# A decode-step kernel (cached attention, then a gated MLP): three buffers for K and V in place of two, a new order of the first loads, and the weights loaded at the end into freed K and V buffers

## Chip, cores, metric

One core of one Trainium2 chip. The metric is device time in microseconds (us), the median of repeated executions. The profile's span is 1.7 to 1.9 us shorter than the time of the same execution. Sums below are made on the spans of the profiled executions unless "time" is said; runs of one kernel differ by 0.2 to 2.2 us, so tenths of a span are worth something only beside a wait that shows the same.

## The reference

```python
# x: 2 x 1 x 512; k_cache, v_cache: 2 x 32 heads x 8192 x 128, bf16
q = (layernorm(x) @ wq)                       # 2 x 32 heads x 128
p = softmax(q . k_cache / sqrt(128))          # over 8192 positions
h = x + (p . v_cache) @ wo                    # wo: 4096 x 512
h2 = h + (relu(ln(h) @ W_gate) * (ln(h) @ W_up)) @ W_down   # 512 x 1376, 1376 x 512
```

K and V are 64 (batch, head) pairs of 2.097 MB each: 268 MB of the 281.7 MB that a run moves. Everything else is small, and comes in smaller rows.

## The kernel before

A pair ("head" below) has its scores computed on VectorE: a product of the K tile (128 partitions x 64 positions x 128) with q, then six halving additions and one last one. ScalarE takes the exponential, TensorE the weighted sum with V. SyncE issues K and the weights on one DMA queue, ScalarE issues V on another.

```python
kt = [sbuf(f"kt{i}", [128, J, Dh]) for i in range(2)]      # two buffers of K; vt the same
...
for i in range(2): dma_v(i)                                # ScalarE's queue
for b in range(B): nc.sync.dma_start(xT[:, :, b], ...)     # x: 1024 elements of 2 bytes
dma_wq_chunk(0); dma_k(0); dma_wq_chunk(1); dma_k(1)       # SyncE's queue
for k in range(2, NWQ): dma_wq_chunk(k)                    # 8 chunks of 0.5 MB, 1 KB rows
...                                                        # layer norm, first q
for i in range(NH):                                        # 64 heads
    nc.vector.wait_ge(kdone[par], 16 * (i // 2 + 1))
    ...
    if i % GH == 1 and g + 1 < NG: emit_q_group_dve(g + 1) # q of 4 heads, PSUM -> SBUF, VectorE
    nc.vector.tensor_tensor(out=prod[:], in0=kt[par][:], in1=qb, op=ALU.mult).then_inc(multdone, 1)
    if i + 2 < NH:
        nc.sync.wait_ge(multdone, i + 1)
        dma_k(i + 2)
        if 2 <= i < 2 + NWT:                               # wo, Wg, Wu, Wd0, Wd1 at heads 2 to 6
            weights_list[i - 2][1]().then_inc(sem_wend, 16)
    ...                                                    # halving tree -> scores
    nc.scalar.activation(out=e_t[par][:], in_=scores[par][:], func=ACT.Exp, ...).then_inc(expdone, 1)
    if i + 2 < NH:
        nc.scalar.wait_ge(pvdone, i + 1)
        dma_v(i + 2)
    ...                                                    # 64 matmuls with V
...                                                        # wo, layer norm, MLP, output
```

The softmax here doesn't subtract the row's maximum and nothing guards it: scores larger than these inputs give would overflow.

## Time and profile before

| | before |
|---|---|
| time, median | 727.66 us (727.13 to 728.16, 13 runs) |
| span of the profiled run | 725.6 us |
| first product starts | 22.74 us |
| last score ends | 705.89 us |
| waits of VectorE for K in the loop | 22.3 us |

The lines on which the reading rests are in the prediction. Two more views. The chain that ended last, shares of the span by engine:

```profile
DVE 80%; DMA 12%; SPq 4%; issue 2%; PE 2%; DVEq 0%; ACT 0%
```

### The profile page before, as it was taken

The page shows a single profiled execution, that of the slowest core. Times are in us where ns is not written, and L with a number is a line of the kernel's source. Part 1 is how long each engine was busy: PE and PEld are TensorE (multiplying, and loading weights), DVE is VectorE, ACT ScalarE, POOL GpSimd, SP SyncE. Part 2 cuts the span into 40 slices and gives each one's busy share as a digit, 9 for nine tenths or more (in the row PEclk, how much of TensorE's full clock was granted, in tenths as well). Part 3 has the DMA queues.
Part 4 walks back from the last instruction along what each step waited for, and adds up shares of the span by engine and source line. Part 5 has one row for each costly group of instructions (what it writes and reads, how often), then busy time and mean ns, then how long its engine had stood idle before and what let it go on. Part 6 is the DMA issues. An engine that isn't in the chain of part 4 may idle for free.

```text
span 725.6 us, 9928 instructions
## 1 busy us (share of the span) xinstructions
PE 158.7 (22%) x4433; PEld 130.2 (18%) x4433; DVE 645.6 (89%) x570; ACT 26.6 (4%) x133; POOL 0.7 (0%) x6
## 2 busy tenths in 40 slices
PE   0312111222123212321323132212321232112216
PEld 0101101112112111210212021201211121111115
DVE  0899188999999999999999999999999999999982
ACT  0000000000000000000000000000000000000010
POOL 0000000000000000000000000000000000000000
DMA  8999999999999999999999999999999999999930
GB/s 342 380 429 396 408 411 411 424 407 399 410 394 416 390 425 385 422 416 391 412 405 421 396 402 406 411 402 403 411 399 426 379 424 406 400 409 399 417 144 3
DMA packets 30348, 281.70 MB, mean 388 GB/s; under 512 B 3329, under 2 KB 12897, under 8 KB 13921
## 3 DMA queue, kind: packets, MB, share of 16 engines
q1 hardware_dynamic: 21088, 146.84, 48.7%
q10 hardware_dynamic: 9216, 134.22, 46.3%
q8 instruction: 35, 0.57, 0.3%
q14 instruction: 9, 0.07, 0.0%
HBM read 281.05 MB, written 0.00 MB: 387 GB/s over the span
## 4 chain that ended last, share of the span: by engine, by line
DVE 80%; DMA 12%; SPq 4%; issue 2%; PE 2%; DVEq 0%; ACT 0%
DVE tb L342 40%; DVE prod L323 36%; DMA kt<-in_A_k_cache_dram 12%; SPq L183 2%; DVE scores L351 2%; SPq L190 1%; DVE qgrp L220 1%; PE work L401 0%; PE work L368 0%; PE work L442 0%; DVEq L319 0%; PE work L448 0%; PE work L471 0%; SPq L241 0%; PE work L386 0%
## 5 line engine op out<-in xcount | busy, mean ns | idle before, releaser
L323 DVE TENSOR_TENSOR prod<-kt,qgrp 128x8192 bf16<-128x8192 bf16 x64 | 283.2, 4426 | 10.0 <-DMA kt<-in_A_k_cache_dram 3.5
L368 PE MATMUL work<-e,vt 128*128 128x1 bf16 x4096 | 119.5, 165 | 539.7 <-ACT e L356 539.7
L368 PEld LDWEIGHTS work<-e,vt 128*128 128x128 bf16 x4096 | 114.2, 104 | 557.3 <-ACT e L356 557.3
L342 DVE TENSOR_TENSOR tb<-tb 128x2048 bf16<-128x2048 bf16 (+4 forms) x320 | 183.0, 572 | 10.9
L342 DVE TENSOR_TENSOR tb<-prod 128x4096 bf16<-128x4096 bf16 x64 | 146.7, 2292 | 2.2
L356 ACT ACTIVATE e<-scores 128x64 bf16<-128x64 f32 x64 | 16.4, 256 | 664.7 <-DVE scores L351 664.7
L209 PE MATMUL qps<-wq_sb,xrep 128*128 128x512 bf16 x64 | 29.9, 623 | 4.5 <-DVEq L297 3.4
L220 DVE CAST qgrp<-qps 128x512 bf16<-128x512 f32 x16 | 11.1, 691 | 22.3 <-DMA kt<-in_A_k_cache_dram 18.8
L351 DVE TENSOR_TENSOR scores<-tb 128x64 f32<-128x64 bf16 x64 | 14.4, 225 | 2.2
L256 DVE CAST xT_f<-xT 128x8 f32<-128x8 bf16 x1 | 0.2, 171 | 14.1 <-DMA xT<-in_A_x_dram 14.1
L356 ACT ACTIVATION_READ_ACCUMULATOR e<-scores 128x1 f32 x64 | 11.9, 186 | 0.0
L209 PEld LDWEIGHTS qps<-wq_sb,xrep 128*128 128x128 bf16 x64 | 6.9, 128 | 14.3 <-issue 8.8
L262 PE MATMUL work<-xT_f,ones_f 128*128 128x8 f32 x2 | 0.6, 370 | 15.5 <-DVE xsq L258 15.5
L401 PE MATMUL work<-O_sb,wo_sb 128*128 128x2 bf16 x128 | 3.6, 165 | 0.6 <-DVEq L395 0.6
L401 PEld LDWEIGHTS work<-O_sb,wo_sb 128*128 128x128 bf16 x128 | 3.5, 104 | 0.8 <-DVEq L395 0.8
L406 DVE TENSOR_TENSOR hT_f<-work,xT_f 128x8 f32<-128x8 f32 x1 | 0.2, 166 | 3.7 <-PE work L401 3.7
L262 PEld LDWEIGHTS work<-xT_f,ones_f 128*128 128x128 f32 x2 | 0.5, 313 | 15.5 <-DVE xsq L258 15.5
L453 DVE COPY u_sb<-work 128x20 f32<-128x20 f32 x1 | 0.2, 179 | 3.1 <-PE work L448 3.1
L382 DVE RECIPROCAL zinv<-work 1x64 f32<-1x64 f32 x1 | 0.5, 546 | 2.6 <-PE work L378 2.6
L442 PE MATMUL work<-hnT,Wg_sb 128*128 128x2 bf16 (+1 forms) x44 | 1.5, 170 | 2.2 <-DVEq L436 2.2
L442 PEld LDWEIGHTS work<-hnT,Wg_sb 128*128 128x128 bf16 (+1 forms) x44 | 1.5, 112 | 2.3 <-DVEq L436 2.3
L448 PE MATMUL work<-hnT,Wu_sb 128*128 128x2 bf16 (+1 forms) x44 | 1.5, 170 | 0.0
(55 smaller groups left out, 21.3 us busy)
## 6 DMA issues: line engine op xcount, KB each, us to landing
vt<-in_A_v_cache_dram ACTq DMA_DIRECT2D x64, 2048.0 KB, 12.6
kt<-in_A_k_cache_dram SPq DMA_DIRECT2D x64, 2048.0 KB, 12.9
wq_sb<-in_A_wq_dram SPq DMA_DIRECT2D x8, 512.0 KB, 14.4
wo_sb<-in_A_wo_dram SPq DMA_DIRECT2D x1, 4096.0 KB, 39.0
Wg_sb<-in_B_W_gate_dram SPq DMA_DIRECT2D x1, 1376.0 KB, 19.5
Wu_sb<-in_B_W_up_dram SPq DMA_DIRECT2D x1, 1376.0 KB, 21.0
Wd_sb<-in_B_W_down_dram SPq DMA_DIRECT2D x1, 1280.0 KB, 19.6
Wd_sb<-in_B_W_down_dram SPq DMA_DIRECT2D x1, 96.0 KB, 19.9
```

The lines of the kernel that those rows point to most:

```text
L183: return nc.sync.dma_start(wq_sb[:, :, k * GW:(k + 1) * GW], A_wq[:, k * GW:(k + 1) * GW].rearrange("(c p) n -> p c n", p=128),).then_inc( ...
L190: return nc.sync.dma_start(kt[i % 2][:], A_k_cache[b, h].rearrange("(p j) d -> p j d", p=128)).then_inc(kdone[i % 2], 16)
L209: last = nc.tensor.matmul(qps[:, slot * 512:slot * 512 + GW], lhsT=xrep[:, b_g * DC + c, :], rhs=wq_sb[:, c, col0:col0 + GW], start=(c == ...
L220: dve.run(nc.vector.tensor_copy(out=q_grp[slot][:], in_=qps[:, slot * 512:slot * 512 + GW]))
L323: nc.vector.tensor_tensor(out=prod[:], in0=kt[par][:], in1=qb, op=ALU.mult).then_inc(multdone, 1)
L342: dve.run(nc.vector.tensor_tensor(out=out_ap, in0=cur_in[:, :, 0:half], in1=cur_in[:, :, half:cur_w], op=ALU.add))
L351: nc.vector.tensor_tensor(out=scores[par][:], in0=cur_in[:, :, 0:1].rearrange("p j o -> p (j o)"), in1=cur_in[:, :, 1:2].rearrange("p j o ...
L356: nc.scalar.activation(out=e_t[par][:], in_=scores[par][:], func=ACT.Exp, scale=inv_sqrt_dh, accum_out=ZP[:, col:col + 1]).then_inc(expdon ...
L368: last = nc.tensor.matmul(O_ps[:, col:col + 1], lhsT=vt[par][:, j, :], rhs=e_t[par][:, j:j + 1], start=(j == 0), stop=(j == NJ - 1))
L401: last = nc.tensor.matmul(attnT_ps[:, ncx * B:(ncx + 1) * B], lhsT=wo_sb[:, h, ncx * 128:(ncx + 1) * 128], rhs=O_sb[:, h, :], start=(h == ...
L442: last = nc.tensor.matmul(g_ps[0:fw, fc * B:(fc + 1) * B], lhsT=Wg_sb[:, c, fc * 128:fc * 128 + fw], rhs=hnT[:, c, :], start=(c == 0), sto ...
L448: last = nc.tensor.matmul(u_ps[0:fw, fc * B:(fc + 1) * B], lhsT=Wu_sb[:, c, fc * 128:fc * 128 + fw], rhs=hnT[:, c, :], start=(c == 0), sto ...
```

## The change

Intent: let the DMA engines run further ahead, keep the early part free of weights that are needed only at the end, and let x and K0 come first. V is issued one head ahead up to head 20 and two ahead afterwards. Wg, Wu and Wd have no memory of their own any more: they are loaded into K and V buffers that are free at the end.

```diff
+    NB = 3                                   # kt, vt, kdone, vdone: i % NB in place of i % 2
-                for i in range(min(2, NH)):
-                    dma_v(i)
                 (x)
                 dma_wq_chunk(0)
                 dma_k(0)
-                if NWQ > 1: dma_wq_chunk(1)
-                if NH > 1: dma_k(1)
-                for k in range(2, NWQ): dma_wq_chunk(k)
+                dma_wq_chunk(1)
+                dma_k(1)
+                dma_wq_chunk(2)
+                dma_k(2)
                 (layer norm)
+                nc.scalar.wait_ge(kdone[0], 16)
+                dma_v(0)
 (loop)
-                    if i + 2 < NH:
+                    if i + NB < NH:
                         nc.sync.wait_ge(multdone, i + 1)
-                        dma_k(i + 2)
-                        if 2 <= i < 2 + NWT:
-                            weights_list[i - 2][1]().then_inc(sem_wend, 16)
+                        dma_k(i + NB)
+                        if i % 4 == 1 and 3 + i // 4 < NWQ: dma_wq_chunk(3 + i // 4)
+                        if i == 60: (wo).then_inc(sem_wo, 16)
 (exponential)
+                    if i >= 2: nc.scalar.wait_ge(pvdone, i - 1)      # before the exponential
-                    if i + 2 < NH:
-                        nc.scalar.wait_ge(pvdone, i + 1)
-                        dma_v(i + 2)
+                    if i < 20: dma_v(i + 1)
+                    elif i == 20: dma_v(i + 1); nc.scalar.wait_ge(pvdone, i); dma_v(i + 2)
+                    elif i + 2 < NH: nc.scalar.wait_ge(pvdone, i); dma_v(i + 2)
 (after the loop)
+                nc.sync.wait_ge(multdone, NH - 2); (Wg into kt of head 61)
+                nc.sync.wait_ge(multdone, NH - 1); (Wu into kt of head 62)
+                nc.sync.wait_ge(pvdone, NH - 2);   (Wd into vt of head 61)
```

More of the change, by code (lines that the diff above doesn't have):

```diff
@@ L61, in bass_sequential_preLN__gqa_block_cached__glu_gated_reglu__decode_kernel @@
     qdim = Hq * Dh
-    GH = 4
-    assert Hq % GH == 0
+    GH = 4 if Hq % 4 == 0 else Hq
     NGB = Hq // GH
@@ L73, in bass_sequential_preLN__gqa_block_cached__glu_gated_reglu__decode_kernel @@
         sem_x = S("x")
-        sem_wq2 = None
-        sem_wend = S("wend")
+        sem_wo = S("wo")
+        sem_wgu = S("wgu")
+        sem_wd = S("wd")
         sem_prep = S("prep")
@@ L80, in bass_sequential_preLN__gqa_block_cached__glu_gated_reglu__decode_kernel @@
         sem_qcopied = S("qcopied")
-        kdone = [S("kdone0"), S("kdone1")]
-        vdone = [S("vdone0"), S("vdone1")]
+        kdone = [S(f"kdone{k}") for k in range(NB)]
+        vdone = [S(f"vdone{k}") for k in range(NB)]
         multdone = S("multdone")
@@ L110, in bass_sequential_preLN__gqa_block_cached__glu_gated_reglu__decode_kernel @@
         dve = EngChain(nc.vector, dvesem)
-        kt = [es.enter_context(nc.sbuf_tensor(f"kt{i}", [128, J, Dh], BF16)) for i in range(2)]
-        vt = [es.enter_context(nc.sbuf_tensor(f"vt{i}", [128, J, Dh], BF16)) for i in range(2)]
+        kt = [es.enter_context(nc.sbuf_tensor(f"kt{i}", [128, J, Dh], BF16)) for i in range(NB)]
+        vt = [es.enter_context(nc.sbuf_tensor(f"vt{i}", [128, J, Dh], BF16)) for i in range(NB)]
         wq_sb = es.enter_context(nc.sbuf_tensor("wq_sb", [128, DC, qdim], BF16))
@@ L117, in bass_sequential_preLN__gqa_block_cached__glu_gated_reglu__decode_kernel @@
         wo_sb = es.enter_context(nc.sbuf_tensor("wo_sb", [128, Hq, D], BF16))
-        Wg_sb = es.enter_context(nc.sbuf_tensor("Wg_sb", [128, DC, F], BF16))
-        Wu_sb = es.enter_context(nc.sbuf_tensor("Wu_sb", [128, DC, F], BF16))
-        Wd_sb = es.enter_context(nc.sbuf_tensor("Wd_sb", [128, FC, D], BF16))
         ones_f32 = es.enter_context(nc.sbuf_tensor("ones_f32", [128, 128], F32))
@@ L150, in bass_sequential_preLN__gqa_block_cached__glu_gated_reglu__decode_kernel @@
         e_t = [es.enter_context(nc.sbuf_tensor(f"e{i}", [128, J], BF16)) for i in range(2)]
+        if DC * F <= J * Dh and FC * D <= J * Dh and NH >= 3:
+            alias_w = True
+            pstride = kt[0][:].ap[0]
+            wg_view = bass.AP(kt[(NH - 3) % NB], 0, [[pstride[0], 128], [F, DC], [1, F]])
+            wu_view = bass.AP(kt[(NH - 2) % NB], 0, [[pstride[0], 128], [F, DC], [1, F]])
+            wd_view = bass.AP(vt[(NH - 3) % NB], 0, [[pstride[0], 128], [D, FC], [1, D]])
+        else:
+            alias_w = False
+            wg_t = es.enter_context(nc.sbuf_tensor("wg_sb", [128, DC, F], BF16))
+            wu_t = es.enter_context(nc.sbuf_tensor("wu_sb", [128, DC, F], BF16))
+            wd_t = es.enter_context(nc.sbuf_tensor("wd_sb", [128, FC, D], BF16))
+            wg_view = wg_t[:]
+            wu_view = wu_t[:]
+            wd_view = wd_t[:]
         qps = es.enter_context(nc.psum_tensor("qps", [128, 2 * 512], F32))
@@ L168, in bass_sequential_preLN__gqa_block_cached__glu_gated_reglu__decode_kernel @@
         sem_wq = [S(f"wq{k}") for k in range(NWQ)]
-        weights_list = [
-            ("wo", lambda: nc.sync.dma_start(wo_sb[:], A_wo.rearrange("(h d) n -> d h n", d=128))),
-            ("Wg", lambda: nc.sync.dma_start(Wg_sb[:], B_W_gate.rearrange("(c p) f -> p c f", p=128))),
-            ("Wu", lambda: nc.sync.dma_start(Wu_sb[:], B_W_up.rearrange("(c p) f -> p c f", p=128))),
-        ]
         nfull = F // 128
         frem = F - nfull * 128
-        weights_list.append(("Wd0", lambda: nc.sync.dma_start(
-            Wd_sb[:, 0:nfull, :], B_W_down[0:nfull * 128, :].rearrange("(c p) n -> p c n", p=128))))
-        if frem:
-            weights_list.append(("Wd1", lambda: nc.sync.dma_start(Wd_sb[0:frem, nfull, :], B_W_down[nfull * 128:F, :])))
-        wend_total = 16 * len(weights_list)
         def dma_wq_chunk(k):
@@ L190, in dma_k @@
             return nc.sync.dma_start(
-                kt[i % 2][:], A_k_cache[b, h].rearrange("(p j) d -> p j d", p=128)
-            ).then_inc(kdone[i % 2], 16)
+                kt[i % NB][:], A_k_cache[b, h].rearrange("(p j) d -> p j d", p=128)
+            ).then_inc(kdone[i % NB], 16)
         def dma_v(i):
@@ L196, in dma_v @@
             return nc.scalar.dma_start(
-                vt[i % 2][:], A_v_cache[b, h].rearrange("(p j) d -> p j d", p=128)
-            ).then_inc(vdone[i % 2], 16)
+                vt[i % NB][:], A_v_cache[b, h].rearrange("(p j) d -> p j d", p=128)
+            ).then_inc(vdone[i % NB], 16)
         def emit_q_group_pe(g):
@@ L245, in _ @@
                 dma_k(0)
-                if NWQ > 1:
-                    dma_wq_chunk(1)
-                if NH > 1:
-                    dma_k(1)
-                for k in range(2, NWQ):
-                    dma_wq_chunk(k)
+                dma_wq_chunk(1)
+                dma_k(1)
+                dma_wq_chunk(2)
+                dma_k(2)
                 dve.run(nc.vector.memset(ones_f32[:], 1.0))
@@ L305, in _ @@
                 NJ = J
-                NWT = len(weights_list)
                 for i in range(NH):
                     b, h = divmod(i, Hq)
+                    buf = i % NB
                     par = i % 2
@@ L312, in _ @@
                     gslot = g % 2
-                    if i % GH == 0 and 1 <= g + 1 < NG and i > 0:
-                        pass
-                    nc.vector.wait_ge(kdone[par], 16 * (i // 2 + 1))
+                    nc.vector.wait_ge(kdone[buf], 16 * (i // NB + 1))
                     if i >= 1:
@@ L323, in _ @@
                     nc.vector.tensor_tensor(
-                        out=prod[:], in0=kt[par][:], in1=qb, op=ALU.mult).then_inc(multdone, 1)
-                    if i + 2 < NH:
+                        out=prod[:], in0=kt[buf][:], in1=qb, op=ALU.mult).then_inc(multdone, 1)
+                    if i + NB < NH:
                         nc.sync.wait_ge(multdone, i + 1)
-                        dma_k(i + 2)
-                        if 2 <= i < 2 + NWT:
-                            weights_list[i - 2][1]().then_inc(sem_wend, 16)
+                        dma_k(i + NB)
+                        if i % 4 == 1 and 3 + i // 4 < NWQ:
+                            dma_wq_chunk(3 + i // 4)
+                        if i == 60:
+                            nc.sync.dma_start(wo_sb[:], A_wo.rearrange("(h d) n -> d h n", d=128)).then_inc(sem_wo, 16)
                     nc.vector.wait_ge(multdone, i + 1)
@@ L336, in _ @@
                         half = cur_w // 2
-                        buf = tb1 if toggle == 0 else tb2
-                        out_ap = buf[:, 0:J * half].rearrange("p (j w) -> p j w", w=half)
+                        bt = tb1 if toggle == 0 else tb2
+                        out_ap = bt[:, 0:J * half].rearrange("p (j w) -> p j w", w=half)
                         if not first:
@@ L355, in _ @@
                     nc.scalar.wait_ge(sready, i + 1)
+                    if i >= 2:
+                        nc.scalar.wait_ge(pvdone, i - 1)
                     nc.scalar.activation(
@@ L358, in _ @@
                         accum_out=ZP[:, col:col + 1]).then_inc(expdone, 1)
-                    if i + 2 < NH:
-                        nc.scalar.wait_ge(pvdone, i + 1)
+                    if i < 20:
+                        dma_v(i + 1)
+                    elif i == 20:
+                        dma_v(i + 1)
+                        nc.scalar.wait_ge(pvdone, i)
+                        dma_v(i + 2)
+                    elif i + 2 < NH:
+                        nc.scalar.wait_ge(pvdone, i)
                         dma_v(i + 2)
@@ L364, in _ @@
                     nc.tensor.wait_ge(expdone, i + 1)
-                    nc.tensor.wait_ge(vdone[par], 16 * (i // 2 + 1))
+                    nc.tensor.wait_ge(vdone[buf], 16 * (i // NB + 1))
                     last = None
@@ L368, in _ @@
                         last = nc.tensor.matmul(
-                            O_ps[:, col:col + 1], lhsT=vt[par][:, j, :], rhs=e_t[par][:, j:j + 1],
+                            O_ps[:, col:col + 1], lhsT=vt[buf][:, j, :], rhs=e_t[par][:, j:j + 1],
                             start=(j == 0), stop=(j == NJ - 1))
                     last.then_inc(pvdone, 1)
-                n_emitted = max(0, min(NWT, NH - 4))
-                for w in range(n_emitted, NWT):
-                    weights_list[w][1]().then_inc(sem_wend, 16)
+                if alias_w:
+                    nc.sync.wait_ge(multdone, NH - 2)
+                nc.sync.dma_start(wg_view, B_W_gate.rearrange("(c p) f -> p c f", p=128)).then_inc(sem_wgu, 16)
+                if alias_w:
+                    nc.sync.wait_ge(multdone, NH - 1)
+                nc.sync.dma_start(wu_view, B_W_up.rearrange("(c p) f -> p c f", p=128)).then_inc(sem_wgu, 16)
+                if alias_w:
+                    nc.sync.wait_ge(pvdone, NH - 2)
+                nc.sync.dma_start(
+                    wd_view[:, 0:nfull, :], B_W_down[0:nfull * 128, :].rearrange("(c p) n -> p c n", p=128)
+                ).then_inc(sem_wd, 16)
+                wd_total = 16
+                if frem:
+                    nc.sync.dma_start(wd_view[0:frem, nfull, :], B_W_down[nfull * 128:F, :]).then_inc(sem_wd, 16)
+                    wd_total = 32
                 nc.tensor.wait_ge(expdone, NH)
@@ L396, in _ @@
                 nc.tensor.wait_ge(sem_osb, 1)
-                nc.tensor.wait_ge(sem_wend, wend_total)
+                nc.tensor.wait_ge(sem_wo, 16)
                 last = None
@@ L437, in _ @@
                 nc.tensor.wait_ge(sem_hn, 1)
+                nc.tensor.wait_ge(sem_wgu, 32)
                 last = None
@@ L442, in _ @@
                         last = nc.tensor.matmul(
-                            g_ps[0:fw, fc * B:(fc + 1) * B], lhsT=Wg_sb[:, c, fc * 128:fc * 128 + fw],
+                            g_ps[0:fw, fc * B:(fc + 1) * B], lhsT=wg_view[:, c, fc * 128:fc * 128 + fw],
                             rhs=hnT[:, c, :], start=(c == 0), stop=(c == DC - 1))
@@ L448, in _ @@
                         last = nc.tensor.matmul(
-                            u_ps[0:fw, fc * B:(fc + 1) * B], lhsT=Wu_sb[:, c, fc * 128:fc * 128 + fw],
+                            u_ps[0:fw, fc * B:(fc + 1) * B], lhsT=wu_view[:, c, fc * 128:fc * 128 + fw],
                             rhs=hnT[:, c, :], start=(c == 0), stop=(c == DC - 1))
@@ L466, in _ @@
                 nc.tensor.wait_ge(sem_hd, 1)
+                nc.tensor.wait_ge(sem_wd, wd_total)
                 last = None
@@ L471, in _ @@
                         last = nc.tensor.matmul(
-                            yT_ps[:, ncx * B:(ncx + 1) * B], lhsT=Wd_sb[0:fw, fc, ncx * 128:(ncx + 1) * 128],
+                            yT_ps[:, ncx * B:(ncx + 1) * B], lhsT=wd_view[0:fw, fc, ncx * 128:(ncx + 1) * 128],
                             rhs=hd[0:fw, fc * B:(fc + 1) * B], start=(fc == 0), stop=(fc == FC - 1))
```

## The prediction

> **What bounds the kernel now.** I read the page first: busy shares and slices. Format of the rows: tenths of each slice that an engine was busy, 40 slices of 18.1 us.
>
> ```profile
> PE 158.7 (22%) x4433; PEld 130.2 (18%) x4433; DVE 645.6 (89%) x570; ACT 26.6 (4%) x133; POOL 0.7 (0%) x6
> ...
> DVE  0899188999999999999999999999999999999982
> ...
> DMA  8999999999999999999999999999999999999930
> GB/s 342 380 429 396 408 411 411 424 407 399 410 394 416 390 425 385 422 416 391 412 405 421 396 402 406 411 402 403 411 399 426 379 424 406 400 409 399 417 144 3
> ```
>
> VectorE and the DMA engines are both full nearly everywhere. VectorE has three holes: slice 1, slices 5 to 7, and the end. DMA has none until the last 30 us. Next, the groups by shape, for what one head costs on VectorE:
>
> ```profile
> L323 DVE TENSOR_TENSOR prod<-kt,qgrp 128x8192 bf16<-128x8192 bf16 x64 | 283.2, 4426 | 10.0 <-DMA kt<-in_A_k_cache_dram 3.5
> L342 DVE TENSOR_TENSOR tb<-prod 128x4096 bf16<-128x4096 bf16 x64 | 146.7, 2292 | 2.2
> L342 DVE TENSOR_TENSOR tb<-tb 128x2048 bf16<-128x2048 bf16 x64 | 78.3, 1224 | 2.2
> ```
>
> With the five smaller steps (692, 425, 292, 226, 225 ns) a head is 9.80 us of work; the distance from one product to the next in the timeline is 10.13 us, and 10.97 us when a group of q is copied first (15 times inside the loop). So the loop without waits is 64 x 10.13 + 15 x 0.84 = 660.9 us. The waits of VectorE (us in total, times, longest) say what is added:
>
> ```profile
> DVE qgrp L220 <- DMA kt<-in_A_k_cache_dram: 18.8, 2, 18.5
> DVE xT_f L256 <- DMA xT<-in_A_x_dram: 14.1, 1, 14.1
> ...
> DVE prod L323 <- DMA kt<-in_A_k_cache_dram: 3.5, 2, 2.4
> ```
>
> The first product starts at 22.74 and the last score ends at 705.89: 683.15 us, which is 660.9 plus 22.3 of waits for K. The two holes have their cause in the timeline (start, duration[...]):
>
> ```profile
> 0.74 1.00 SPq L241 DMA_DIRECT2D xT<-in_A_x_dram  x2
> 0.75 1.00 ACTq L196 DMA_DIRECT2D vt<-in_A_v_cache_dram  x2
> ...
> 2.32 9.17 SPq L190 DMA_DIRECT2D kt<-in_A_k_cache_dram  x1
> ...
> 15.12 0.17 DVE L256 CAST xT_f<-xT 128x8 f32<-128x8 bf16 x1 [14.12 <-DMA xT<-in_A_x_dram]
> ...
> 59.48 18.07 SPq L190 DMA_DIRECT2D kt<-in_A_k_cache_dram  x1
> ...
> 93.72 0.69 DVE L220 CAST qgrp<-qps 128x512 bf16<-128x512 f32 x1 [18.52 <-DMA kt<-in_A_k_cache_dram]
> ```
>
> x (1024 packets of 2 bytes) is issued together with two V loads and lands only at 15; K of head 5 stands behind wo (4 MB in 1 KB rows, issued at 49.7) and its issue alone takes 18 us. Last, the same counters over long stretches (last two columns: DMA share, GB/s):
>
> ```profile
> 140.00:570.00 430.00, 95.13 (x2668) 76.89 (x2665) 414.71 (x341) 14.30 (x82) 0.00 (x0) 1.00 0.99 406
> 35.00:60.00 25.00, 5.55 (x136) 3.93 (x132) 23.26 (x18) 0.70 (x4) 0.00 (x0) 1.00 1.01 425
> ```
>
> In the steady part VectorE sets the pace: four heads take 3 x 10.13 + 10.97 = 41.36 us and ask for 8 x 2.097 MB, 406 GB/s, which is what DMA delivers. When both queues have a backlog it delivers 425. So the reserve of the DMA engines is some 4%, no more: that is the number on which this case turns.
>
> **What the Trainium skill says.** "DMA: Bandwidth & Descriptors", section "Queues, rings and completion order": each DMA engine goes round between the queues that have work, a packet at a time. The packet records agree: between 3 and 13 us each half microsecond starts about 12 packets of V (16 KB, 611 ns) and about 12 of x (2 bytes, 9 ns), one for one; in the half microsecond after V ended, 396 packets of x start. So a queue with small packets is slowed to the pace of the big ones beside it. The section "Issuing engines are not separate DMA queues" says that queues of different engines share the same 16 DMA engines; the trace agrees, the sum never goes past some 440 GB/s. "HBM Reference", "Specifications", says that a core streaming alone measures about 425 GB/s, bounded by its DMA engines; the 425 above agrees. "Perfetto Trace Analysis", "Identifying the Most-Contended Engine", calls the occupancy of 16 DMA engines misleading; here too, since 0.99 busy goes with 406 and with 425.
>
> **The change part by part.** No instruction of VectorE, TensorE or ScalarE is added or removed: the order of instructions per engine is the same but for DMA issues. What changes is when 281.7 MB are asked for, and in how many buffers.
>
> *Start.* V0 and V1 no longer go ahead of x; V0 waits for K0. x is then alone: the records show 59 packets in its first quarter microsecond and 88 in the next half, before V came in full; at about 250 per us, 1024 take 4 us from 1.8, so it is through at 6 and lands at 7. From x's landing to the first product the old kernel needs 22.74 - 15.12 = 7.6 us (layer norm, q), so 14.4. K0: wq0 takes 1.6 us (some 170 packets of 1 KB each half us), K0 5.2 us, landing 0.7: 6 + 7.5 = 13.5, in time. First product at about 14.4 in place of 22.7: 8.4 us gained, all on the path.
>
> *The hole at 75 to 94.* wo, Wg, Wu, Wd (8.3 MB) leave the early heads, and five of eight wq chunks are spread over heads 1 to 17. The 22.3 us of K waits go with the queue that made them. But the reserve is thin. Four heads and a wq chunk are 16.8 MB at 420 GB/s, 39.9 us, and 1.5 us for the chunk: 41.4 against VectorE's 41.36. So in the first 17 heads there is no lead to be built, and whatever is short at the start stays: K1 and V0 share the engines, then wq2 stands among V1's packets one for one (up to 5 us during which K does not move), then K2: I follow K1 to land at 24.0 (wanted at 24.5), K2 at 36.4 (35.5), K5, behind wq3, at 69.5 (66.7). Together I set 4 us of new waits. Triple buffers do not add bandwidth; they only let K be asked for 10 us earlier, so they absorb a late one such as the K of 16 us at 577 in the old kernel (0.3 us of wait there).
>
> *Steady part.* VectorE-bound as before, 41.36 us per four heads. The lead grows by about 0.2 to 0.4 us a head, so by head 60 K is its full two to three buffers ahead. Nothing gained, nothing lost. The new wait of the exponential for the weighted sum two heads back is no new wait in time: the sum follows the exponential within 2.5 us.
>
> *Tail.* wo is issued after the product of head 60 (time T), Wg, Wu, Wd after it into freed K and V buffers. Scores of head 63 end at T + 5.7 + 30.4 + 0.8 = T + 36.9. Old tail: from score end 705.9 to wo's first matmul 4.6 us, to Wg's 11.9, to Wd's 15.5, to the end 19.7. So wanted: wo T + 41.5, Wg and Wu T + 48.8, Wd T + 52.4. To be moved from T on, in time of the engines: rest of K62 1 to 5 us, K63 5, rest of V61 3, V62 and V63 5 each, wo 13 (256 rows of 1 KB per engine at 51 ns), Wg and Wu 3.5 each (109 ns a row), Wd 4.4: 43 to 48 us. Add 2 for issue and landing: wo at T + 34 to 40, Wu at T + 41 to 46, Wd at T + 45 to 50. They arrive just in time; I set 1.5 us for lateness.
>
> *Sum.* 727.4 - 8.4 - 22.3 + 4 + 1.5 = 702.2 us.
>
> **The rivals.** *DMA becomes the bound.* Two floors lie close: VectorE's 14.4 + 660.9 + 19.7 = 695.0 us of span, and DMA's: 6 us of start, then 281.7 MB, at 425 GB/s 663 and at 406 694 us, then 5.7 us from Wd's last byte to the end: 675 to 706. If the true rate with both queues always full is nearer 406 (the steady part never showed whether it could go faster), the holes come back as small waits for K all along, and the time is some 708. For it: DMA share 0.99 over 430 us. Against: 425 to 440 in several 5 us windows, and no wait for K over 48 heads with double buffers. *The weights come late at the end*: at 406 GB/s the tail's reserve is gone and TensorE waits 3 to 9 us for Wg or Wd: 705 to 710. *The start does not gain*: if x, 2 bytes a packet, is slow by itself, the first product stays near 20 and the time is 708. *K's queue is starved by its own wq chunks* in heads 2 to 17: 8 us more than I set, 710. Against the last: what V takes early it does not take later, since V is issued one head at a time.
>
> **Range and chances.** All rivals but a combination of two end under 712.9, which is 2% faster. Low end: no new waits at all, 696. High end: one rival in full and half of another, 711. Faster by over 2%: 0.93; within 2%: 0.06; slower: 0.01.
>
> **What would show it.** x landing near 7 and the first product near 14.4 show the start right. The wait of the q copy for K falls from 18.8 to under 5, and waits for K lie before 200 us only. The steady stretch again shows 406 GB/s and 41.36 us per four heads. The last score ends near 680 and no matmul waits over 3 us for a weight. I am wrong if waits for K spread over the whole run (DMA bound), if the chain at the end runs through wo, Wg or Wd loads, or if VectorE's 4426 ns product gets longer.

## More of the kernel before

All profiled runs here are at a granted clock of 1.0.

DMA issues of the kernel before (name, issuing queue, count, KB each, median us from issue to landing):

```profile
vt<-in_A_v_cache_dram ACTq DMA_DIRECT2D x64, 2048.0 KB, 12.6
kt<-in_A_k_cache_dram SPq DMA_DIRECT2D x64, 2048.0 KB, 12.9
wq_sb<-in_A_wq_dram SPq DMA_DIRECT2D x8, 512.0 KB, 14.4
wo_sb<-in_A_wo_dram SPq DMA_DIRECT2D x1, 4096.0 KB, 39.0
```

VectorE carries four fifths of the chain; the DMA and SyncE-queue shares are the start, the waits for K at heads 2, 5 and 8 and one late K at 577 us; the largest is the hole at head 5, behind wo, whose 4 MB took 39 us to land while K and V of 2 MB take 13.

## The result

The changed kernel takes 695.44 us, median of 8 runs (694.75 to 695.77), against 727.66: a ratio of 0.9558, 95% interval 0.9548 to 0.9567. Ratios here are the mean time of one kernel's fast runs over that of the other's of the same rounds, so not quite the ratio of the medians. The direction and the size class were predicted; the time lies 0.6 us under the range.

The page of the changed kernel, the rows that answer to those in the prediction:

```profile
PE 158.1 (23%) x4433; PEld 130.3 (19%) x4433; DVE 645.5 (93%) x570; ACT 26.6 (4%) x133; POOL 0.7 (0%) x6
...
DVE  5999999999999999999999999999999999999982
...
DMA  8999999999999999999999999999999999999992
GB/s 337 420 425 425 425 421 423 421 430 419 429 426 419 426 428 429 426 427 429 425 428 426 425 410 419 410 406 416 382 423 396 414 422 386 407 408 409 397 386 64
...
DVE 90%; DMA 4%; issue 2%; PE 2%; DVEq 0%; ACT 0%; SPq 0%
```

VectorE's busy time is the same, 645.5 us; only the holes are gone. DMA is full to the end and moves 419 to 430 GB/s from slice 2 to slice 23, where the kernel before moved 380 to 429. The start, in the timeline:

```profile
0.74 0.99 SPq L242 DMA_DIRECT2D xT<-in_A_x_dram  x2
...
4.25 0.17 DVE L255 CAST xT_f<-xT 128x8 f32<-128x8 bf16 x1 [3.25 <-DMA xT<-in_A_x_dram]
...
10.83 0.38 ACTq L199 DMA_DIRECT2D vt<-in_A_v_cache_dram  x1
...
11.87 4.42 DVE L323 TENSOR_TENSOR prod<-kt,qgrp 128x8192 bf16<-128x8192 bf16 x1
```

x lands at 4.2 in place of 15.1, K0 at 10.8 in place of 21.5, and the first product starts 10.87 us earlier. VectorE's one remaining wait for K in the whole loop, where there had been 18.8 and 3.5 us:

```profile
DVE qgrp L223 <- DMA kt<-in_A_k_cache_dram: 0.9, 1, 0.9
```

The end, again the timeline (first matmuls with wo, Wg and Wd; in brackets what ended the idle time before them):

```profile
678.48 3.57 PE L423 MATMUL work<-O_sb,wo_sb 128*128 128x2 bf16 x128 [0.64 <-DVEq L417]
...
685.75 1.55 PE L465 MATMUL work<-hnT,kt 128*128 128x2 bf16 x44 [2.21 <-DVEq L458]
...
689.35 1.33 PE L495 MATMUL work<-hd,vt 128*128 128x2 bf16 x44 [0.67 <-DVEq L488]
```

All three wait for VectorE, none for a load: wo had landed at 670.3, Wu at 677.3, Wd at 681.6. The last score ends at 673.86 and the end is 19.7 us later, as before.

So the 32.0 us of span divide into 10.87 at the start, 21.16 in the loop (683.15 us from first product to last score became 661.99) and nothing at the end. What stays is VectorE: 661.99 us are its 660.9 of bare work and spacing plus 1.1.

### The profile page after: what moved, and what is told of

It is laid out like the page before. It is cut to its first block, busy times and chain, and to the rows that moved or that the text cites. A ratio compares the mean times of both kernels' runs of the same rounds, so it can differ in the third digit from the quotient of the medians.

```text
span 693.6 us, 9992 instructions
## 1 busy us (share of the span) xinstructions
PE 158.1 (23%) x4433; PEld 130.3 (19%) x4433; DVE 645.5 (93%) x570; ACT 26.6 (4%) x133; POOL 0.7 (0%) x6
## 4 chain that ended last, share of the span: by engine, by line
DVE 90%; DMA 4%; issue 2%; PE 2%; DVEq 0%; ACT 0%; SPq 0%
DVE tb L344 46%; DVE prod L323 40%; DMA kt<-in_A_k_cache_dram 4%; DVE scores L353 2%; DVE qgrp L223 2%; PE work L423 1%; DMA xT<-in_A_x_dram 0%; PE qps L212 0%; PE work L378 0%; DVEq L319 0%; PE work L465 0%; PE work L471 0%; PE work L495 0%; DVE xrep L292 0%; PE work L408 0%
## 5 line engine op out<-in xcount | busy, mean ns | idle before, releaser
L465 PE MATMUL work<-hnT,kt 128*128 128x2 bf16 (+1 forms) x44 | 1.5, 170 | 2.2 <-DVEq L458 2.2
L465 PEld LDWEIGHTS work<-hnT,kt 128*128 128x128 bf16 (+1 forms) x44 | 1.5, 112 | 2.3 <-DVEq L458 2.3
L471 PE MATMUL work<-hnT,kt 128*128 128x2 bf16 (+1 forms) x44 | 1.5, 170 | 0.0
```

The source lines that it names most:

```text
L465: last = nc.tensor.matmul(g_ps[0:fw, fc * B:(fc + 1) * B], lhsT=wg_view[:, c, fc * 128:fc * 128 + fw], rhs=hnT[:, c, :], start=(c == 0), s ...
L471: last = nc.tensor.matmul(u_ps[0:fw, fc * B:(fc + 1) * B], lhsT=wu_view[:, c, fc * 128:fc * 128 + fw], rhs=hnT[:, c, :], start=(c == 0), s ...
```

## The experiments

All kernels gave results within the tolerance. Times are medians, each against the kernel before in the same rounds (727.3 to 727.4 us; 727.66 for the changed kernel).

| run | what differs | time us | ratio to before | first product | waits for K in the loop |
|---|---|---|---|---|---|
| changed kernel | | 695.44 | 0.9558 | 11.87 | 0.9 |
| e1_start | before + new start only | 732.01 | 1.0065 | 11.71 | 39.2 |
| e11_weights_late | before + weights at the end only | 706.26 | 0.9708 | 22.86 | 1.1 |
| e2_loads | e11 + wq spread | 705.48 | 0.9698 | 22.76 | none |
| e5_v_first | changed - new start | 705.52 | 0.9695 | 22.84 | none |
| e4_wo_early | changed, wo at head 2 | 712.53 | 0.9795 | 11.75 | 18.1 |
| e6_wq_front | changed, all wq before K2 | 707.32 | 0.9720 | 11.78 | 12.9 |
| e3_two_buffers | e2 + new start, V0 and V1 together | 700.47 | 0.9633 | 11.89 | 5.4 |
| e9_v1_with_v0 | changed, V0 and V1 together | 695.00 | 0.9555 | 11.87 | 0.5 |
| e10_two_buffers_v1_late | e3, V1 after the first exponential | 703.14 | 0.9664 | 11.88 | 8.8 |
| e12_two_buffers_v_paced | e3, V one head ahead to head 20 | 696.13 | 0.9568 | 11.79 | 2.2 |
| e7_light | changed, tree cut short (wrong on purpose) | 678.76 | 0.9330 | 11.84 | 176.8 |
| e8_q_on_act | changed, q copied by ScalarE | 685.68 | 0.9428 | 11.59 | 3.5 |

My theory after the result: the order in which small-row loads stand in K's queue is the whole of the loop's gain, the early start is the rest, and the third buffer gives little. Rivals: the buffers carry the gain; the parts simply add up; DMA is the bound of the changed kernel.

### One part at a time, on the kernel before

```diff
 # e1_start                                # e11_weights_late
-for i in range(min(2, NH)): dma_v(i)      -if 2 <= i < 2 + NWT: weights_list[i - 2]...
 ...layer norm...                          +if i == NH - 3: all of weights_list, a semaphore each
+nc.scalar.wait_ge(kdone[0], 16)           # e2_loads: e11, and
+dma_v(0); dma_v(1)                        +wq chunks 0 to 2 first, then one each at heads 1, 5, 9, 13, 17
```

> The old kernel with the start alone changed: V0 and V1 wait for K0, two buffers and all early loads as before. If the parts simply add up, the first product comes at 11.9 us in place of 22.7 and the time falls by 10.9 us, to about 716.7 us. If the DMA engines are the common limit of the first 100 us (they are full there in the old kernel), K of head 5 cannot land sooner, the hole of 18.5 us grows by about what the start gains, and the time stays at 725 to 729 us.

> The old kernel with the weights alone moved to the end (a semaphore each), all wq chunks still up front, V0 and V1 first, two buffers. If wo in front of K5 was the cause of the hole, the wait of 18.4 us at head 5 and that of 2.3 at head 8 go and the 1.0 at head 2 stays: 705 to 709 us. If the wq burst has a part in the hole: over 712 us.

> The old kernel with the loads alone moved: wq spread over heads 1 to 17, the weights behind the last K with a semaphore each, V0 and V1 still first, two buffers. If the early queue made the 22.3 us of waits for K, they go: the first product stays at 22.7 us, waits for K are under 3 us, time 704 to 708 us. If two buffers are too few for a DMA with so thin a reserve, waits for K come back and the time is over 712 us.

e1 is slower than the kernel before: 732.01 us, by 0.65% (interval 0.50 to 0.80%). Its first product starts 11 us earlier, and all of it is given back and more. Waits of VectorE for K, then the stretch 35 to 60 us (PE, PEld, DVE, ACT, POOL busy, clock, DMA share, GB/s):

```profile
DVE prod L324 <- DMA kt<-in_A_k_cache_dram: 24.1, 2, 19.2
DVE qgrp L220 <- DMA kt<-in_A_k_cache_dram: 15.1, 2, 13.4
```

```profile
35.00:60.00 25.00, 0.03 (x1) 0.00 (x0) 7.95 (x4) 0.00 (x0) 0.00 (x0) 1.00 0.92 354
```

The kernel before moved 425 GB/s in that stretch. Here K2 lands at 51.9 us, where it landed at 44.9 before, although its buffer is free 11 us sooner. Between K1 and K2 stand six wq chunks in 1 KB rows, in the same queue: K2 was issued behind them, at 33.7 (29.6 before). Before, V0 and V1 had passed ahead of x and the chunks ran nearly alone (wq7 landed at 36.9). Now V0 to V3 run beside them, packet for packet, and wq7 lands at 47.0. (This is read from the packet records; no run isolates it.) My expectation had the sign of the rival right ("time stays"), but not that it would lose 4.6 us: the parts do not add up.

e11 moves wo, Wg, Wu and Wd together: the waits at heads 5 and 8 are gone, the one at head 2 stays, and the span falls by 20.8 us (725.6 to 704.8). That wo is the one that makes the hole is shown by e4 below, which puts wo alone back. The only wait for K in e11:

```profile
DVE prod L323 <- DMA kt<-in_A_k_cache_dram: 1.1, 1, 1.1
```

e2 takes that last microsecond as well (span 703.7), still with two buffers. So in the old start the burst of wq chunks cost 1 us, and two buffers were enough for a loop without waits.

### The start undone, and the bursts put back, with three buffers

```diff
 # e5_v_first: changed kernel       # e4_wo_early          # e6_wq_front
+for i in range(2): dma_v(i)        -if i == 60: (wo)      -dma_wq_chunk(2)
 (x)                                +if i == 2: (wo)       +for k in range(2, NWQ): dma_wq_chunk(k)
-wait kdone[0]; dma_v(0)                                    dma_k(2)
+(no dma_v at i == 0)                                      -(one chunk at heads 1, 5, 9, 13, 17)
```

> The changed kernel with V0 and V1 issued first again, ahead of x. x lands at about 15 us and the first product starts at 22.7; nothing else to wait for: 10.9 us more than the changed kernel, 705 to 708 us. If later slack took the start in (DMA as the bound), it would be under 700 us.

> The changed kernel with wo (4 MB) issued after the product of head 2 in place of head 60, three buffers. K of head 6 then stands behind 13 us of wo and V packets beside it: a wait of 8 to 18 us at head 6, time 703 to 713 us. If the third buffer takes the burst in: under 698 us.

> The changed kernel with all eight wq chunks issued in front of K2. wq2 to wq7 are 3 MB of 1 KB packets that go one for one with V0 and V1: K2 comes some 8 to 14 us late, time 702 to 710 us. If three buffers took it in: under 698 us.

e5 has the span of e2 to the tenth, 703.7 us, without a wait for K: the start is worth 10.1 us when the loads are in order, and in that start the third buffer gives nothing. e4 and e6 (waits for K, one line of each kernel):

```profile
DVE prod L323 <- DMA kt<-in_A_k_cache_dram: 17.0, 1, 17.0
```

```profile
DVE prod L324 <- DMA kt<-in_A_k_cache_dram: 12.9, 1, 12.9
```

Three buffers do not take in a burst of small rows. wo at head 2 makes head 6 wait 17.0 us, nearly the 18.5 of the kernel before at head 5, only one head later. The packet records of e4 show 25 rows of wo a microsecond beside V's 24 (68 to 70 us) and 340 when V is quiet (74 to 76). No run loads wo in larger rows, so what the row size costs and what 4 MB in front of K would cost in any form is not separated.

The five extra chunks in e6 make head 2 wait 12.9 us, while the same chunks cost the old start 1 us. That does not mean that they passed more quickly there: K2 landed at 45.7 us in e6, at 44.9 in the kernel before and at 45.0 in e11. But the old start is ready for head 2 only at 43.8 us, e6 at 32.8. The late first product hid the burst; once the start is early, the burst has to move.

### The third buffer

```diff
 # e3: two buffers (e2 + e1)   # e10: e3 but       # e12: e3 but                         # e9: changed kernel but
 wait kdone[0]                 -dma_v(1)           -dma_v(1)                              wait kdone[0]; dma_v(0)
 dma_v(0); dma_v(1)             (exponential 0)     (exponential i, i < 20)              +dma_v(1)
 (exponential i)               +dma_v(1)           +wait pvdone >= i (i >= 1)            +(no dma_v at i == 0)
 wait pvdone >= i + 1                              +dma_v(i + 1)
 dma_v(i + 2)                                       (two ahead from i = 20)
```

> Start and loads changed, but two buffers of K and V in place of three. If the order of the loads is the whole gain, this is within 2 us of the changed kernel, 694 to 697.5 us. If the third buffer carries part of the gain (K cannot be asked for early enough while the start runs just in time), waits for K of 3 to 15 us show in the first 100 us and the time is 699 to 711 us.

> The changed kernel (three buffers), V1 issued right behind V0 in place of after the first exponential. If the 5.3 us of the run with two buffers came of V1 standing in front of K2 (V packets against wq2's small ones, one for one), K2 is late here too: a wait of 2 to 6 us at head 2, time 697.5 to 701 us. If it was the missing third buffer, nothing changes: 694.5 to 696.5 us.

> The run with two buffers, start and loads changed, but V1 issued after the first exponential as the changed kernel does. If the third buffer is worth nothing in time, the wait at head 2 falls under 1.5 us and the time is 694.5 to 697 us. If the third buffer is what spared the changed kernel that wait, it stays at 4 to 6 us and the time is 699 to 702 us.

> Start and loads changed, two buffers, and V issued one head at a time up to head 20 as the changed kernel does (two heads ahead after that). If the 5.3 and 8.7 us of the two runs with two buffers came of V running two heads ahead in the first heads, they go: waits for K under 2.5 us, 695 to 698 us, and the third buffer is worth under 2 us. If K needs the third buffer to be queued in front of the wq chunks, a wait of 4 to 9 us at head 2 or 4 stays: 699 to 704 us.

Waits of VectorE for K, in the order e3, e9, e10, e12:

```profile
DVE prod L321 <- DMA kt<-in_A_k_cache_dram: 5.4, 1, 5.4
```

```profile
DVE prod L324 <- DMA kt<-in_A_k_cache_dram: 0.5, 1, 0.5
```

```profile
DVE prod L320 <- DMA kt<-in_A_k_cache_dram: 8.8, 1, 8.8
```

```profile
DVE prod L320 <- DMA kt<-in_A_k_cache_dram: 2.2, 1, 2.2
```

e3 alone looked as if the third buffer were worth 5 us. e9 and e10 contradicted both simple readings: with three buffers V1 may go early at no cost, and with two buffers holding V1 back made it worse, not better. The packet records show why. In e3 and e9 alike K2's first packet starts at 27.2 or 27.3, once V1 has gone. But in e3 the sum over V0 lets V2 be issued at 24.3 (its first packet is at 28.0) and K2's last packet starts at 36.6; in e9 V2 is issued after the second exponential (at 32.9, first packet at 36.5), K2 has the engines alone and its last packet starts at 32.2. In e10 K2 is in time, but K4 cannot be issued before the product of head 2 and so stands behind chunk wq3; beside V2 and V3, which run back to back from 34.7 to 48.9, no packet of K starts between 39.3 (the last of K3) and 48.3.

e12 is the clean comparison: two buffers, V paced as in the changed kernel. One wait of 2.2 us; 696.13 us against 695.44. The third buffers are worth 0.7 us by the medians, 1.2 by the profiled spans (694.8 against 693.6), with runs that spread over some 1 us each. (e12 also issues wo one head later and has separate memory for the weights; no wait shows for either.) With two buffers, what holds the time is the pacing of V, which keeps V's large packets out of the way of the queue that VectorE waits for.

### What DMA can do

```diff
-while cur_w > 2:     # six halvings
+while cur_w > 64:    # one, wrong on purpose
```

> The changed kernel with five of six halving steps of the tree left out (wrong result on purpose), so that VectorE needs about 7.1 us a head and DMA sets the pace; measures what the DMA engines can do with both queues full. If 420 to 425 GB/s, 281.7 MB take 663 to 671 us and with start and tail the time is 672 to 683 us. If the 406 GB/s of the old steady part was the limit of DMA (rival of the prediction), the time is 698 to 706 us.

VectorE then needs some 7 us a head and waits for K nearly every time. (It passed the comparison all the same, so the comparison is loose for these inputs; it is no valid kernel.) The same stretch in e7 and in the changed kernel:

```profile
140.00:570.00 430.00, 95.97 (x2785) 80.83 (x2796) 303.42 (x138) 14.65 (x84) 0.00 (x0) 1.00 1.01 427
```

```profile
140.00:570.00 430.00, 97.03 (x2732) 78.96 (x2732) 414.53 (x343) 14.30 (x82) 0.00 (x0) 1.00 1.00 420
```

With DMA as the bound the engines give 427 GB/s for 430 us. The rival "406 is DMA's limit" falls. The changed kernel takes 420 in that stretch although VectorE consumes 406: the surplus fills the buffers (and brings wq6 and wq7), and after slice 23 the page's GB/s row falls to a mean of 407, about what VectorE asks for. The floor of DMA in this design is e7's 678.76 us.

### One step further

```diff
-dve.run(nc.vector.tensor_copy(out=q_grp[slot][:], in_=qps[...]))
+nc.scalar.activation(out=q_grp[slot][:], in_=qps[...], func=ACT.Copy).then_inc(sem_qcopied, 1)
+(VectorE waits for sem_qcopied at i % 4 == 0)
```

> The changed kernel with the copy of q from PSUM moved from VectorE to ScalarE, so that four heads need 40.5 us of VectorE and ask DMA for 414 GB/s. If VectorE is the bound of the changed kernel and DMA can do 427, 15 x 0.84 = 12.6 us go: 682 to 686 us. If DMA is already as good as the bound, waits for K take most of it back: 688 to 695 us.

685.68 us, ratio 0.9428 to before, the fastest correct kernel here. Its span is 683.5: 10.1 us under the changed kernel, of the 12.6 that the copies took. The rest is 3.5 us of waits for K in the first heads:

```profile
DVE prod L320 <- DMA kt<-in_A_k_cache_dram: 3.5, 3, 3.1
```

```profile
140.00:570.00 430.00, 96.05 (x2785) 80.74 (x2796) 415.92 (x339) 21.21 (x95) 0.00 (x0) 1.00 1.01 426
```

That shows VectorE as the bound of the changed kernel, and that little is left in DMA: e7's 678.76 us is 6.9 us below. (The 426 GB/s here are not what VectorE asks for, which is 414; as above, the rest fills buffers and brings wq chunks.)

## Why the prediction was right or wrong

**The bound, the two holes and their causes: right.** The waits of 22.3 us and the late x were named as the gain. e11 and e4 together show wo in front of K5 as the cause of the hole, e5 against the changed kernel shows the start. One reading was off: "no wait for K over 48 heads" overlooks the 0.3 us at head 53 in its own account, so it is 44 heads.

**x's landing: the mechanism right, the size wrong.** The step was "at about 250 per us, 1024 take 4 us from 1.8, so it is through at 6 and lands at 7". x landed at 4.2. I took the rate from the first three quarters of a microsecond of the old trace (147 packets, 196 per us, rounded up), where the queue was still starting and V's first packets were already beside it. The better number stood in the prediction itself: 396 packets of x in the half microsecond after V had ended. The records after show 78, 247 and 437 packets of x in the half microseconds from 1.5, 2.0 and 2.5 us. That moved the first product from the predicted 14.4 to 11.87: 2.5 us.

**New waits in the first heads: "Together I set 4 us of new waits" against 1.1 measured.** 2.9 us. The table behind it had K2 landing at 36.4 and K5 at 69.5; they landed at 30.9 and 64.2. It put wq2 among V1's packets. In the run V1 is issued at 21.95, its first packet starts at 25.5, and wq2 had landed at 23.6: it ran beside the end of V0 and then alone. I also reckoned with 420 GB/s where e7 shows 427: four heads and a chunk are then 39.3 + 1.5 = 40.8 us, half a microsecond under VectorE's 41.36 where I had seen no reserve. The danger as such is real: e3 and e10 wait 5.4 and 8.8 us where V runs beside K's queue, and e6 12.9, of which an estimated 7.5 us are the five chunks' own time (1.5 us each when V is quiet, by the landings of wq2 and wq3).

**The tail: "I set 1.5 us for lateness" against nothing.** wo landed 8 us before it was wanted, Wd 7.7 us. The prediction's own table had nothing late (wo by T + 40 against 41.5, Wu by 46 against 48.8, Wd by 50 against 52.4), so the 1.5 us was a margin that its working did not ask for. The engines had moved 420 GB/s in the middle part where I reckoned with what VectorE asks for, 406; that this lead is what made the tail early I read from the rates, no run isolates it.

**The sum.** 2.5 + 2.9 + 1.5 = 6.9 us; 702.2 - 6.9 = 695.3, measured 695.44. Of the three, x's landing is the one that carried the time below the low end: with the waits and the tail put right and the start left as predicted, the sum is 697.8. All three terms erred to the slow side, and the low end of the range ("no new waits at all, 696") took x's landing as certain. The loop's bare 660.9 us (661.2 in e5, which has no wait for K) and the tail's 19.7 held to within 0.3 us: an error bar belonged on the start, not on them.

**The rivals.** "DMA becomes the bound" is refuted by e7 and e8 for this kernel. "The weights come late" and "the start does not gain" did not happen. "K's queue is starved by its own wq chunks" came to 0.9 us here, and to 12.9 with all chunks in front (e6).

**Left out.** I took it that the start gains "all on the path" as a property of its own. It does so only with the loads in order: on the kernel before it costs 4.6 us (e1).

## What to carry to other kernels

When the DMA engines are full nearly all the time, what pays is the order in the queue that the bounding engine waits for: keep large loads in small rows out from in front of its data, and hold back large loads on the other queue that are not needed yet. More buffers of the same size gave about 1 us here, the order and the pacing of V gave over 30 (e12). Judge the worth of a part with the other parts in place: the new start was worth 10.1 us with the loads moved and lost 4.6 us without.

## What the Trainium skill lacked or had wrong

- "DMA: Bandwidth & Descriptors", "Queues, rings and completion order", gives the round of the queues and typical packets of 9 to 17 descriptors, but not what it does to rows of different size. In the records here one 2-byte or 1 KB element goes for one 16 KB row of the other queue: x lands at 15.1 us beside V and at 4.2 alone, and in e6 a wq chunk lands 1.5 us after the one before it with V quiet (wq3), 5.8 us beside V1 (wq5).
- The same page, "Where 436 GB/s comes from", says that for HBM to SBUF the HBM side at about 358 GB/s binds. With one core running, e7 moved 427 GB/s for 430 us. (The same passage goes on to a measured 425, so it contradicts itself for a core alone.) "HBM Reference", with about 425 for a core alone, is right.
- The same page, "Issuing engines are not separate DMA queues", calls the sequencer's time to start a DMA usually small. Issuing K behind wo took 18.07 us on SyncE in the kernel before, and 0.33 us when nothing stood in front. No page that I read says how many rows a queue takes before the issue blocks.
- No page that I read gives a rate for 2-byte elements on this path: up to 437 in half a microsecond over 16 engines here.
- "Perfetto Trace Analysis" is right that DMA occupancy misleads, and the runs say by how much: a share of 0.99 to 1.01 goes with 404 GB/s (e1) and with 427 (e7).
